# Linear attention and two MoE layers on one core: the top-2 gates computed once per 18 tiles instead of in groups of 6 and 3

## The chip, the cores and the metric

The kernel runs on one core of one Trainium2 chip. The metric is the device time of one execution in microseconds; the numbers shown are the median, lowest and highest of three runs, and one further execution was recorded by the profiler. Engines are named as in the profile: PE is TensorE, DVE is VectorE, ACT is ScalarE, POOL is GpSimd, SP is SyncE (it only issues DMAs here).

## What is computed

Linear attention for 8 batches of 8 heads, 576 positions and head size 64, then a top-2 mixture of 8 experts over the 4608 tokens, then a soft mixture. Cut to what matters here:

```python
x = softmax(q) @ (softmax_over_sequence(k).T @ v)        # per head; 4608 tokens x 512
logits = x @ w_gate                                       # 4608 x 8
noisy = logits + log1p(exp(x @ w_noise)) * noise
top2 = argpartition(-noisy, 2)[:, :2]; w = softmax(noisy[top2])
out[t] = sum over the two experts e of t: w * relu(x[t] @ w1[e]) @ w2[e]
# then moe2: soft slots over all tokens, 8 experts x 4 slots
```

The "gate" is the part from `noisy` to the sorted list of tokens for each expert: softplus, the two largest of eight, their weights, a running count for each expert, and a table that says which token stands at which place of which expert's list.

## The kernel before, in words

Tokens are handled in 36 tiles of 128, nine tiles for each of four pairs of batches (`TP` = 9). Tensors live in pools whose tiles have a fixed number of buffers; a second use of a one-buffer tile waits for the first use to end.

`attention` runs steps that two strings name. `FIRST` holds pairs 0, 1 and 2 and the kv product of pair 3; `MIX` holds the outputs of pair 3. `ou1.4` is the output of pair 1, tile 4 (matmuls into a `pv` tile in PSUM, line 308 or 312; evicted by DVE, lines 315 to 328, or with an `a` by ACT, line 324). `qt` transposes q, `kv` makes the kv product (lines 277 and 278), `qm` and `qs` are q's maximum and its subtraction (line 248 on DVE, line 255 mostly on POOL), `he1.2` adds the gate logits over heads for three tiles (line 336), `ga1.0` queues a gate, `pf` queues `plan_first`, `pl` queues `plan`, and each `bg` advances the queued work up to its next mark (a bare `yield`). The written order gives priorities; a planner of the compiler then fixes the order on each engine's queue, so that work may be issued well ahead of its place in the strings. Each engine then runs its queue strictly in that order.

A gate is a chain across four engines. Lines 350 to 370 make the noisy logits (DVE, ACT with exp and log, POOL). Lines 375 to 392 compare the eight values with each other, mask ties and count, so that the two largest get a 1 in `s16`. Lines 395 to 401 are matmuls that give each token its running number per expert, on top of the count `cnt` of all earlier groups. Lines 403 to 409 make the weights and store them to `xtab` in DRAM. Lines 412 to 428 turn numbers into a place (`af` column, `bf` row). Lines 436 to 455 build one-hot matrices of three tiles at a time (`ob` of 128 rows, with the token number multiplied in on line 437; `oa` of `8*T1` columns, line 445) and multiply them into the table; lines 460 to 465 add the result into `tab`. `T1` is the number of the last tile of the group, so `oa` is wider for later groups. Before the change each pair has a group of six tiles and one of three, and one PSUM bank (`pk`) serves the running numbers and the table of every group in turn.

`plan_first` (line 592) needs the whole table of pairs 0 and 1. It makes the index list for the first ten blocks of 256 rows (POOL, line 614) and the first two gathers (line 628). Then `experts` runs: in each block (lines 838 to 870) eight parts, each with one `split` of a weight into two halves (line 763, ACT then DVE), a `hidden` (line 796) or a `result` (line 826) on PE. `MIX` is stretched over the first 72 of the 80 parts of these ten blocks, and ends with `plan`, which needs the whole table and makes the index lists for all later blocks; blocks of 384 rows start after the tenth. The excerpt below is printed from the kernel.

```python
assert i < 2 or TP * (i - 2) + 6 in seen              # before pair i reuses lgr
bg.append(gate(i * TP + 6 * j, i * TP + 6 + 3 * j))   # ga i.j
while n_done < min(n_steps, n_steps * n_parts // SPREAD):   # MIX over the parts
```

## Time and profile before

| | |
|---|---|
| median of three runs | 1232.7 us (1230.85 to 1234.57) |
| the profiled execution's own time | 1234.64 us |
| its span, first to last instruction | 1232.9 us |
| busy: PE, DVE, ACT, POOL | 1148.2, 802.4, 580.7, 326.9 us |
| mean granted TensorE clock | 0.967 of full speed |

The span is what the trace covers; the rest of the profiled execution's time lies around it. Busy time is an average over stages that have different limits, so the stages are read one by one below.

### The profile page before, as it was taken

The numbers are of one execution on the slowest core, as the hardware profiler recorded it, in microseconds if no ns is written. First come the engines' busy times: TensorE is split into PE (matmuls) and PEld (weight loads), VectorE is DVE, ScalarE is ACT, GpSimd is POOL, SyncE is SP. The second block draws the span as 40 slices with busy tenths as digits, with TensorE's granted clock in tenths as the row PEclk, the third lists the DMA queues.
The fourth block names the chain that finished last, engine by engine and source line by source line (L and its number), as shares of the span: only waits on it lengthen the run. The fifth ranks groups of instructions, "written<-read, shape, count | busy, mean of one in ns | idle before, by whom it ended". The sixth has DMA issues, their size and how long they took to land. (4 is left out here: it accounts for less than half of the span.)

```text
span 1232.9 us, 21326 instructions
## 1 busy us (share of the span) xinstructions
PE 1148.2 (93%) x7808; PEld 997.7 (81%) x7808; DVE 802.4 (65%) x1493; ACT 580.7 (47%) x879; POOL 326.9 (27%) x376
## 2 busy tenths in 40 slices
PE   6776989999999999999999999999999999969994
PEld 5665878998888998889978998998998998956542
DVE  7889777678876665555556666666666666646653
ACT  3554666464444444434434454544444454424324
POOL 3353251343242322112222322322321321310000
PEclk9788899999999999999999999999999999988997
DMA  9847471796446475556668564563846353237797
GB/s 342 289 143 274 155 263 40 198 290 186 113 106 180 111 215 148 144 163 169 170 176 264 139 199 104 148 193 85 220 108 171 47 151 78 45 69 287 260 356 307
DMA packets 116107, 219.10 MB, mean 178 GB/s; under 512 B 13968, under 2 KB 54032, under 8 KB 111888
## 3 DMA queue, kind: packets, MB, share of 16 engines
q1 hardware_dynamic: 98944, 177.11, 41.8%
q0 software_dynamic: 17040, 40.44, 17.2%
q8 instruction: 67, 1.10, 0.4%
q14 instruction: 56, 0.46, 0.1%
HBM read 243.31 MB, written 49.70 MB: 238 GB/s over the span
## 5 line engine op out<-in xcount | busy, mean ns | idle before, releaser
L763 DVE TENSOR_TENSOR R1l<-ringS,R1h 128x1024 fp32r<-128x1024 f32 x96 | 117.8, 1227 | 102.7 <-ACT R1h L763 100.2
L763 DVE TENSOR_TENSOR R0l<-ringS,R0h 128x1024 fp32r<-128x1024 f32 x95 | 116.4, 1225 | 104.1 <-ACT R0h L763 103.5
L763 ACT ACTIVATE R1h<-ringS 128x1024 fp32r<-128x1024 f32 x96 | 101.7, 1060 | 141.0 <-PE py L826 85.0
L763 ACT ACTIVATE R0h<-ringS 128x1024 fp32r<-128x1024 f32 x95 | 100.8, 1061 | 138.4 <-PE py L826 75.3
L763 DVE TENSOR_TENSOR R2l<-ringS,R2h 128x1024 fp32r<-128x1024 f32 x91 | 111.4, 1225 | 81.2 <-ACT R2h L763 78.7
L763 ACT ACTIVATE R2h<-ringS 128x1024 fp32r<-128x1024 f32 x91 | 96.5, 1060 | 136.2 <-PE py L826 72.6
L796 PE MATMUL ph<-xh,R0h 128*128 128x256 f32 x400 | 113.3, 283 | 2.5 <-ACT R2h L763 2.4
L796 PE MATMUL ph<-xl,R0h 128*128 128x256 f32 x400 | 113.4, 283 | 0.0
L796 PE MATMUL ph<-xh,R0l 128*128 128x256 f32 x400 | 112.9, 282 | 0.0
L800 DVE SCALAR_TENSOR_TENSOR hl<-ph,hh 128x512 fp32r<-128x512 f32 x140 | 95.7, 684 | 24.0 <-ACT hh L799 24.0
L709 POOL DMA_INDIRECT xg<-xtab,pl_idx x40 | 49.2, 1229 | 216.7 <-DVE sc L786 198.1
L796 PE MATMUL ph<-xh,R2h 128*128 128x256 f32 x360 | 102.2, 284 | 1.9 <-DVE hl L800 1.9
L796 PE MATMUL ph<-xl,R2h 128*128 128x256 f32 x360 | 102.0, 283 | 0.5 <-DVE xl L783 0.5
L796 PE MATMUL ph<-xh,R2l 128*128 128x256 f32 x360 | 101.8, 283 | 0.0
L796 PE MATMUL ph<-xh,R1h 128*128 128x256 f32 x360 | 100.7, 280 | 0.2 <-DVE hl L800 0.2
L796 PE MATMUL ph<-xl,R1h 128*128 128x256 f32 x360 | 100.3, 279 | 0.0
L796 PE MATMUL ph<-xh,R1l 128*128 128x256 f32 x360 | 100.3, 279 | 0.0
L832 POOL DMA_INDIRECT x<-y,pl_idx x40 | 63.5, 1588 | 129.0 <-DVE y L831 118.9
L799 ACT ACTIVATE hh<-ph 128x512 fp32r<-128x512 f32 x140 | 81.6, 583 | 32.5 <-PE ph L796 32.5
L826 PE MATMUL py<-R1l,hh 128*128 128x512 f32 x200 | 79.7, 399 | 0.0
L796 PEld LDWEIGHTS ph<-xh,R0h 128*128 128x128 f32 x400 | 76.2, 191 | 3.8 <-ACT R2h L763 2.8
L826 PE MATMUL py<-R1h,hl 128*128 128x512 f32 x200 | 78.8, 395 | 0.0
(439 smaller groups left out, 3064.6 us busy)
## 6 DMA issues: line engine op xcount, KB each, us to landing
ringS<-in_moe_w_dram SPq DMA_DIRECT2D x292, 512.0 KB
ringA<-in_moe_w_dram SPq DMA_DIRECT2D x12, 1024.0 KB
ringA<-in_moe_w_dram SPq DMA_DIRECT2D x22, 512.0 KB
xtab<-xr SPq DMA_DIRECT2D x36, 256.0 KB
kt<-in_k_dram SPq DMA_DIRECT2D x8, 1024.0 KB
v<-in_v_dram SPq DMA_DIRECT2D x8, 1024.0 KB
x<-z SPq DMA_DIRECT2D x5, 1280.0 KB
ringS<-x SPq DMA_DIRECT2D x5, 1024.0 KB
```

The costliest lines, as they stand in the source:

```text
L709: k.nc.gpsimd.indirect_dma_start(out=x, out_offset=None, in_=k.xtab[:n], in_offset=bass.IndirectOffsetOnAxis(ap=idx, axis=0))
L763: turn[1:] = [nc.scalar.activation(r[0], f, AF.Copy), nc.vector.tensor_sub(r[1], f, r[0].bitcast(F32))]
L796: nc.tensor.matmul(ph[:, g, :], w[i][:, c, g * P:(g + 1) * P], x[:, c, :], start=n == 0, stop=n == 11)
L799: nc.scalar.activation(hh[:, fs, :], ph, AF.Relu)
L800: nc.vector.scalar_tensor_tensor(hl[:, fs, :], ph, 0.0, hh[:, fs, :].bitcast(F32), op0=ALU.max, op1=ALU.subtract)
L826: nc.tensor.matmul(py[s], a[h], w[i][:, f, :], start=u == 4 and f == n == 0, stop=u == 7 and f == 1 and n == 2)
L832: d = nc.gpsimd.indirect_dma_start(out=k.x2[:NTOK // 2] if b < NPA else k.x2, out_offset=bass.IndirectOffsetOnAxis(ap=at(b, s), axis=0), i ...
```

## The change

Both kernels do the same arithmetic on the same tokens. `gate(i)` now takes 18 tiles, two pairs, and is queued twice: `ga0` in `FIRST` after `he1.2`, `ga2` in `MIX` after `he3.2`. The 58 `bg` of `FIRST` become 31: none stands ahead of `ga0`, and behind it one follows nearly every step (`he1.2 ga0 bg qe2.2 bg kv2.0 bg km3.0 bg kv2.0 bg kt2.0 bg ...`), 26 of them ahead of `pf` and 5 behind it, the last after `ke3.1`. All other steps keep their order. `MIX` has 105 entries in place of 85, with the outputs of pair 3 in the first 25. `heads` writes its last sum into a new tile `ls` of 18 tiles. The comparison `ge` is made in fp16, and its mask is multiplied on DVE and no longer on POOL. The one-hot matrices are made three tiles at a time with two buffers, and the table is made in two halves of nine tiles; `oa` has 144 columns for all of the first gate and 288 for all of the second. Names such as `g0` let intermediate tiles share memory.

```diff
 NPA, NPB, NST, NTR = 10, 30, 14, 8
 TE = 36
 NSLOT = 32
-GT = 6
+
+GN, GT = 2 * TP, TP
...
 MIX = """
-ga2.0 ga2.1 qt3.0 bg bg bg bg bg ou3.0a qt3.1 bg bg bg qt3.2 bg ou3.1a bg qt3.3 ou3.2 bg qt3.4 bg he3.0 ou3.3 bg qt3.5 bg ou3.4 bg bg bg bg ze ze qt3.6 bg ze bg ou3.5a bg bg qt3.7 bg bg ze he3.1 ou3.6a bg ou3.7 qt3.8 ou3.8 bg bg bg bg bg bg bg he3.2 bg bg bg ga3.0 bg ga3.1 bg bg bg bg pl bg bg bg bg bg bg bg bg bg bg bg bg bg bg bg
+qt3.0 ou3.0a qt3.1 qt3.2 ou3.1a qt3.3 ou3.2 qt3.4 he3.0 ou3.3 qt3.5 ou3.4 ze ze qt3.6 ze ou3.5a qt3.7 ze he3.1 ou3.6a ou3.7 qt3.8 ou3.8 he3.2 ga2 bg bg bg bg bg bg bg bg bg bg bg bg bg bg bg bg bg bg bg bg bg bg bg bg bg bg bg bg bg bg bg bg bg bg bg bg bg bg bg bg bg bg bg bg bg bg bg bg bg bg bg bg bg bg bg bg bg bg bg bg bg bg bg bg bg bg bg bg bg bg pl bg bg bg bg bg bg bg bg
 """
...
-    k.tril = ap.tile([P, E, E], F32, name="tril")
-    nc.gpsimd.affine_select(out=k.tril, in_=k.ones[:, :64].rearrange("p (e f) -> p e f", e=E), pattern=[[1, E], [-1, E]], compare_op=ALU.is_gt, fill=0.0, base=0, channel_multiplier=0)
+    trf = ap.tile([P, E, E], F32, name="trf")
+    nc.gpsimd.affine_select(out=trf, in_=k.ones[:, :64].rearrange("p (e f) -> p e f", e=E), pattern=[[1, E], [-1, E]], compare_op=ALU.is_gt, fill=0.0, base=0, channel_multiplier=0)
+    k.tril = ap.tile([P, E, E], F16, name="tril")
+    nc.vector.tensor_copy(k.tril, trf)
...
         def heads(T0, T1, eng):
 
-            lr = lgrs[T0 // TP][:, T0 % TP:T0 % TP + T1 - T0]
-            for w in (4, 2, 1):
+            i, j = T0 // TP, T0 % TP
+            lr = lgrs[i][:, j:j + T1 - T0]
+            for w in (4, 2):
                 eng.tensor_add(lr[:, :, 0:w], lr[:, :, 0:w], lr[:, :, w:2 * w])
-
-        def gate(T0, T1):
-            n_t = T1 - T0
+            if i // 2 not in lss:
+                lss[i // 2] = sp.tile([P, GN, 2 * E], F32, name="ls")
+            j += i % 2 * TP
+            eng.tensor_add(lss[i // 2][:, j:j + T1 - T0], lr[:, :, 0], lr[:, :, 1])
+            seen.append(T0)
+
+        def gate(i):
+
+            T0, n_t = i * TP, GN
+            T1 = T0 + n_t
 
 
             n_c = E * T1
             cols = k.cols[:, :n_c]
             tabs = tab.rearrange("p (e c) -> p e c", e=E)[:, :, :T1]
-            full = lambda n, s=None, d=F32: sp.tile(s or [P, GT, E], d, name=n)[:, :n_t]
+            full = lambda n, s=None, d=F32: sp.tile(s or [P, GN, E], d, name=n)
             flat = lambda x: x.rearrange("p t e -> p (t e)")
-            lr = lgrs[T0 // TP][:, T0 % TP:T0 % TP + n_t]
-            z = lr[:, :, 0, E:]
-            na = full("na")
+            lr = lss[i // 2]
+            z = lr[:, :, E:]
+            na = full("g0")
             nc.vector.scalar_tensor_tensor(na, z, -1.0, z, op0=ALU.mult, op1=ALU.min)
-            u = full("u")
+            u = full("g1")
             nc.scalar.activation(u, na, AF.Exp)
...
-            n = sp.tile([P, GT, E], F32, name="n", bufs=2)[:, :n_t]
+            n = full("n")
             nc.gpsimd.tensor_mul(n, ln, noise[:, T0:T1, :])
-            nc.gpsimd.tensor_add(n, n, lr[:, :, 0, 0:E])
-            yield 1
-            seen.append(T0)
-
-            ge = full("ge", [P, GT, E, E])
+            nc.gpsimd.tensor_add(n, n, lr[:, :, 0:E])
+            yield
+
+            ge = full("ge", [P, GN, E, E], F16)
             nc.vector.tensor_tensor(ge, bcast(n, 2, E), bcast(n, 3, E), op=ALU.is_ge)
             yield 1
-            nc.gpsimd.tensor_tensor(ge, ge, bcast(k.tril, 1, n_t), op=ALU.mult)
-            m1 = full("m1", [P, GT])
+            nc.vector.tensor_tensor(ge, ge, bcast(k.tril, 1, n_t), op=ALU.mult)
+            m1 = full("m1", [P, GN])
             nc.vector.tensor_reduce(m1, n, axis=AX.X, op=ALU.max)
             nc.gpsimd.tensor_sub(n, n, bcast(m1, 2, E))
             nc.scalar.activation(n, n, AF.Exp)
             yield
...
-            pk = pr.tile([P, GT, E], F32, name="pk")[:, :n_t]
+            pk = pr.tile([P, GN, E], F32, name="pk")
...
-            ob = sp.tile([P, GT, P, 2], F16, name="ob")
-            parts = [slice(m, m + CW // 2) for m in range(0, n_t, CW // 2)]
             over = lambda x, ms, n: bcast(x[:, ms], 2, n)
-            for ms in parts:
-                n_p = ms.stop - ms.start
-                nc.vector.tensor_tensor(ob[:, ms], bcast(k.cols[:, :P], 1, n_p), over(bf, ms, P), op=ALU.is_equal)
-                nc.vector.tensor_tensor(ob[:, ms], ob[:, ms], over(k.tok1, ms, P), op=ALU.mult)
-                yield 1
-            yield
-            oas = []
-
-            def columns(ms):
-                n_p = ms.stop - ms.start
-                oas.append(sp.tile([P, CW // 2, E * TE, 2], F16, name="oa", bufs=2)[:, :n_p, :n_c])
-                nc.vector.tensor_tensor(oas[-1], bcast(cols, 1, n_p), over(af, ms, n_c), op=ALU.is_equal)
-
-            for ms in parts[:2]:
-                columns(ms)
-                yield 1
-            yield
-            pa = pr.tile([P, E, T1], F32, name="pk")
-            for ms in parts:
-                oa = oas.pop(0)
-                for m in range(2 * ms.start, 2 * ms.stop):
-                    nc.tensor.matmul(pa.rearrange("p e c -> p (e c)"), ob[:, m // 2, :, m % 2], oa[:, m // 2 - ms.start, :, m % 2], start=m == 0, stop=m == 2 * n_t - 1)
-                if len(oas) and ms.stop < n_t - CW // 2:
-                    columns(slice(ms.stop + CW // 2, ms.stop + CW))
+            for h in range(0, n_t, GT):
+                pa = pr.tile([P, E, T1], F32, name="pk")
+                for m0 in range(0, GT, CW // 2):
+                    ms, ml = slice(h + m0, h + m0 + CW // 2), slice(m0, m0 + CW // 2)
+                    ob = sp.tile([P, CW // 2, P, 2], F16, name="ob", bufs=2)
+                    nc.vector.tensor_tensor(ob, bcast(k.cols[:, :P], 1, CW // 2), over(bf, ms, P), op=ALU.is_equal)
+                    yield 1
+                    nc.vector.tensor_tensor(ob, ob, over(k.tok1, ml, P), op=ALU.mult)
+                    yield 1
+                    oa = sp.tile([P, CW // 2, E * TE, 2], F16, name="oa", bufs=2)[:, :, :n_c]
+                    nc.vector.tensor_tensor(oa, bcast(cols, 1, CW // 2), over(af, ms, n_c), op=ALU.is_equal)
+                    for m in range(CW):
+                        nc.tensor.matmul(pa.rearrange("p e c -> p (e c)"), ob[:, m // 2, :, m % 2], oa[:, m // 2, :, m % 2], start=m0 + m == 0, stop=m0 + CW // 2 == GT and m == CW - 1)
+                    yield
+                if T0 + h == 0:
+                    nc.vector.tensor_copy(tabs, pa)
+                else:
+                    tt = sp.tile([P, E * TE], F32, name="tt")[:, :n_c].rearrange("p (e c) -> p e c", e=E)
+                    nc.vector.tensor_scalar(tt, pa, 0.0, float((T0 + h) * P), op0=ALU.is_gt, op1=ALU.mult)
+                    nc.vector.tensor_add(tabs, tabs, pa)
+                    nc.vector.tensor_add(tabs, tabs, tt)
                 yield
-            if T0 == 0:
-                nc.vector.tensor_copy(tabs, pa)
-            else:
-                tt = sp.tile([P, E * TE], F32, name="tt")[:, :n_c].rearrange("p (e c) -> p e c", e=E)
-                nc.vector.tensor_scalar(tt, pa, 0.0, float(T0 * P), op0=ALU.is_gt, op1=ALU.mult)
-                nc.vector.tensor_add(tabs, tabs, pa)
-                nc.vector.tensor_add(tabs, tabs, tt)
...
-                bg.append(gate(i * TP + 6 * j, i * TP + 6 + 3 * j))
+                bg.append(gate(i))
```

## Rows read from the trace of the kernel before

**Rows 1.** Stretches: length, busy PE, PEld, DVE, ACT, POOL (instructions), PEclk, DMA, GB/s

```profile
106.00:131.00 25.00, 15.39 (x94) 12.77 (x93) 23.41 (x68) 12.31 (x29) 10.97 (x11) 0.66 0.69 249
131.00:143.00 12.00, 12.00 (x81) 10.06 (x82) 7.45 (x29) 4.76 (x7) 5.61 (x18) 1.00 0.65 231
143.00:169.00 26.00, 21.64 (x184) 19.49 (x185) 24.95 (x98) 20.60 (x58) 6.23 (x14) 1.00 0.34 123
169.00:182.00 13.00, 13.00 (x97) 11.06 (x96) 7.20 (x29) 7.25 (x17) 8.92 (x25) 1.00 0.93 310
182.00:194.00 12.00, 8.97 (x62) 8.00 (x62) 11.89 (x41) 6.82 (x12) 5.05 (x7) 0.86 0.47 150
194.00:250.00 56.00, 56.00 (x385) 51.59 (x384) 37.97 (x77) 28.86 (x50) 13.23 (x14) 1.00 0.45 124
...
300.00:345.00 45.00, 42.92 (x290) 38.71 (x289) 37.87 (x92) 22.86 (x29) 18.32 (x20) 1.00 0.46 113
...
445.00:625.00 180.00, 180.00 (x1185) 163.31 (x1185) 93.60 (x147) 74.03 (x116) 38.80 (x29) 1.00 0.58 159
```

**Rows 2.** Waits of PE, 60 to 131 us, by releaser: total us, times, longest

```profile
PE pv L312 <- DVE lgr L328: 4.3, 1, 4.3
PE pk L395 <- DVE tab L460: 3.4, 1, 3.4
PE pk L455 <- DVE ob L437: 2.2, 1, 2.2
PE pv L277 <- ACT xr L324: 2.0, 1, 2.0
```

**Rows 3.** Timeline of DVE: start, us, line; first and last gate instructions of four stretches

```profile
68.35 2.75 DVE L350 SCALAR_TENSOR_TENSOR na<-lgr 128x48 f32<-128x48 f32 x1 [0.38 <-POOL lgr L336]
...
130.15 0.44 DVE L362 RECIPROCAL rw<-w 128x48 f32<-128x48 f32 x1
...
168.62 0.29 DVE L465 TENSOR_TENSOR tab<-tab,tt 128x144 f32<-128x144 f32 x1
...
193.90 0.17 DVE L407 RECIPROCAL s<-s 128x3 f32<-128x3 f32 x1
...
337.06 0.45 DVE L465 TENSOR_TENSOR tab<-tab,tt 128x288 f32<-128x288 f32 x1
```

**Rows 4.** Timeline of POOL: a subtraction of q, gathers, the plan's last copy

```profile
68.27 2.76 POOL L255 TENSOR_TENSOR q<-q,qm 128x1536 f32<-128x1536 f32 x1
...
178.99 1.19 POOL L709 DMA_INDIRECT pl_x<-xtab,pl_ia  x1 [1.10 <-DMA ringS<-in_moe_w_dram]
...
355.15 0.18 POOL L688 COPY pl_id<-pl_idx 128x2 int32 x1 [0.27 <-POOL pl_idx L684]
...
420.57 1.02 POOL L709 DMA_INDIRECT xg<-xtab,pl_id  x1 [14.31 <-PE py L826]
```

**Rows 5.** Timeline of PE: outputs, the first gathered rows, the first expert matmul

```profile
95.52 1.27 PE L308 MATMUL pv<-KB,qT 128*128 128x162 f32 x8
...
118.05 2.53 PE L308 MATMUL pv<-KB,qT 128*128 128x162 f32 x8 [0.54 <-DVE lgr L328]
...
186.43 1.92 PE L781 MATMUL ph<-ident,pl_x 128*128 128x128 f32 x8
...
193.83 0.36 PE L796 MATMUL ph<-xh,R1h 128*128 128x256 f32 x1
```

**Rows 6.** Gate instructions of DVE by shape, to 445 us: busy us, mean ns

```profile
L437 DVE TENSOR_TENSOR ob<-ob,tok 128x768 f16<-128x768 f16 x12 | 6.7, 579 | 0.0
L387 DVE TENSOR_REDUCE r<-ge 128x48 f32<-128x384 f32 x4 | 3.4, 850 | 0.0
...
L387 DVE TENSOR_REDUCE r<-ge 128x24 f32<-128x192 f32 x4 | 2.0, 492 | 0.0
...
L445 DVE TENSOR_TENSOR oa<-cols,af 128x1728 f16<-128x1728 f16 x1 | 1.1, 1066 | 0.0
...
L445 DVE TENSOR_TENSOR oa<-cols,af 128x864 f16<-128x864 f16 x1 | 0.6, 594 | 0.0
```

More of the change, by code (lines that the diff above doesn't have):

```diff
@@ L146, in attention @@
         lgrs, rqas, seen = {}, {}, []
-        m8s = {}
+        m8s, lss = {}, {}
         tab = k.tab = ac.tile([P, E * TE], F32, name="tab")
@@ L344, in gate @@
             tabs = tab.rearrange("p (e c) -> p e c", e=E)[:, :, :T1]
-            full = lambda n, s=None, d=F32: sp.tile(s or [P, GT, E], d, name=n)[:, :n_t]
+            full = lambda n, s=None, d=F32: sp.tile(s or [P, GN, E], d, name=n)
             flat = lambda x: x.rearrange("p t e -> p (t e)")
-            lr = lgrs[T0 // TP][:, T0 % TP:T0 % TP + n_t]
-            z = lr[:, :, 0, E:]
-            na = full("na")
+            lr = lss[i // 2]
+            z = lr[:, :, E:]
+            na = full("g0")
             nc.vector.scalar_tensor_tensor(na, z, -1.0, z, op0=ALU.mult, op1=ALU.min)
-            u = full("u")
+            u = full("g1")
             nc.scalar.activation(u, na, AF.Exp)
-            w = full("w")
+            w = full("g2")
             nc.vector.tensor_scalar_add(w, u, 1.0)
@@ L357, in gate @@
             yield
-            dl = full("dl")
+            dl = full("g0")
             nc.vector.scalar_tensor_tensor(dl, w, -1.0, u, op0=ALU.add, op1=ALU.subtract)
-            rw = full("rw")
+            rw = full("g3")
             nc.vector.reciprocal(rw, w)
@@ L382, in gate @@
             yield
-            r1 = full("r1")
+            r1 = full("g1")
             nc.vector.tensor_reduce(r1, ge, axis=AX.X, op=ALU.add)
             yield
-            r2 = full("r2")
+            r2 = full("g2")
             nc.vector.tensor_reduce(r2, ge.rearrange("p t e f -> p t f e"), axis=AX.X, op=ALU.add)
-            yield 1
+            yield
             nc.vector.tensor_sub(r1, r1, r2)
@@ L403, in gate @@
             nc.gpsimd.tensor_mul(n, n, s16)
-            s = full("s", [P, GT])
+            s = full("s", [P, GN])
             nc.vector.tensor_reduce(s, n, axis=AX.X, op=ALU.add)
@@ L410, in gate @@
             yield
-            pos = full("pos")
+            pos = full("g0")
             nc.vector.scalar_tensor_tensor(pos, bcast(k.ef, 1, n_t), float(T1 * P), pk, op0=ALU.mult, op1=ALU.add)
             nc.vector.tensor_mul(pos, pos, s16)
-            pp = full("pp", [P, GT, 2])
+            pp = full("pp", [P, GN, 2])
             nc.vector.tensor_reduce(pp[:, :, 1], pos, axis=AX.X, op=ALU.max)
             yield 1
-            ps = full("ps", [P, GT])
+            ps = full("ps", [P, GN])
             nc.vector.tensor_reduce(ps, pos, axis=AX.X, op=ALU.add)
@@ L420, in gate @@
             yield
-            pi = full("pi", [P, GT, 2], I32)
+            pi = full("pi", [P, GN, 2], I32)
             nc.vector.tensor_copy(pi, pp)
-            ai = full("ai", [P, GT, 2], I32)
+            ai = full("ai", [P, GN, 2], I32)
             nc.vector.tensor_scalar(ai, pi, 7, None, op0=ALU.logical_shift_right)
-            af = full("af", [P, GT, 2], F16)
+            af = full("af", [P, GN, 2], F16)
             nc.vector.tensor_copy(af, ai)
-            bf = full("bf", [P, GT, 2], F16)
+            bf = full("bf", [P, GN, 2], F16)
```

4 lines of the change are left out of this document (2 added, 2 removed).

## The prediction

> **What bounds the kernel now.** I read the chain that ended last first. It can be followed back only to the start of the blocks of 256 rows behind 625 us, and there it is expert matmuls. The table of stretches fills in the rest: from 445 to 625 us PE is busy for all of its 180 us at full clock, and from 194 to 250 for all of 56 [rows 1]. So the end is set by when PE gets through the first ten blocks, and what happens after 445 us moves as a whole. Only idle PE, a slow PE clock or added PE work ahead of 445 us counts.
>
> Read in the same table, the attention stage is different. From 106 to 131 us PE is busy for 15.39 of 25 us, DVE for 23.41, and the granted clock is 0.66. Then PE is full in both kv products (131 to 143 and 169 to 182), where DVE has 7.45 of 12 and 7.20 of 13 us of work. Between them DVE is the full engine, with 24.95 of 26, and again from 182 to 194, with 11.89 of 12 [rows 1]. The stage is bound in turn by DVE, PE, DVE, PE, DVE.
>
> Next, the waits of PE show what the gate of pair 0 costs there. PE waits 2.2 us for a one-hot matrix and 3.4 us for the table before the PSUM bank is free, with outputs of pair 1 queued behind both. It waits 4.3 us for an eviction that stands in DVE's queue behind the first gate instruction, and 2.0 us for an ACT eviction whose factor stands behind another [rows 2]. That first gate instruction lasts 2.75 us for 48 elements [rows 3], as long as the POOL subtraction that started 0.08 us before it [rows 4]. The outputs that follow cost PE 2.53 us in place of 1.27 us [rows 5], at about half the clock: a granted 1.2 GHz where it was 2.4.
>
> **The change, part by part.** *DVE work.* Counting the gate's lines 350 to 465, DVE spends 27.6 us on 67 instructions up to the reciprocal at 130.15, 18.6 us on 64 from there to the table at 168.62, 14.1 us on 45 up to 193.90 and 26.6 us on 85 up to 337.06 [rows 3]. For a group of 18 tiles I take the slopes of the shapes. The second sum over `ge` grows by 0.358 us for three more tiles, so 0.850 + 4 x 0.358 = 2.28 us. A chunk of three tiles takes 0.58 + 0.58 + 0.594 = 1.75 us for `ob` twice and `oa` in the first gate, and 0.58 + 0.58 + 1.066 = 2.23 in the second [rows 6]; six chunks are 10.5 and 13.4 us. I put the other 25 small instructions at 10 us and the table at 1.1 and 2.7 us, an estimate on the same slopes. That makes about 24 us for the first gate and 28 us for the second. Ahead of the experts the gate's DVE work thus falls from 27.6 + 18.6 + 14.1 = 60.3 to about 24 us, since pair 2's gate is moved behind pair 3's outputs; behind their start it grows from 26.6 to about 28.
>
> *Up to the end of pair 1 (131 us).* All gate work leaves. The gate's share of the waits is 2.2 + 3.4 + 2.0, and of the 4.3 us the 2.7 that the blocked instruction took: 10.3 us. The slow clock added 1.26 us to each of three outputs; with half of that, 1.9, the stretch could shrink by 12. Other work is late next: from 106 to 131 DVE still has about 12 us (its 23.41 less some 11 that I count of the gate's 27.6), and the ACT evictions and POOL subtractions remain. I take -9 us. Bounds: -5, the waits for `ob` and half of the rest; -14, all of it and the whole clock loss.
>
> *From there to the experts.* The first gate's 24 us stands where 18.6 us of pair 1's stood: +5.4 us for DVE, plus waits of a chain that cannot overlap with another group of its own. The kv stretches can hide some: DVE idles 4.6 us in the first [rows 1]. I take +4 us, bounds 0 and +8. The first expert block hangs on the table: from it (168.62) to the gather 10.4 us, to the transposes of the gathered rows 17.8, to the first expert matmul 25.2 [rows 3 to 5]. In that last piece, 182 to 194, DVE is full, with pair 2's gate on it and PE idle for 3.0 us [rows 1]. Without that gate the splits come sooner: -2 us; bounds -5, and +3 if the longer chain has the table later than now and PE runs out of pair 3's outputs to fill with.
>
> *Behind the experts' start.* Six small groups of waits and table loads become one chain, but it can only use gaps of DVE, 18 of 56 us in the stretch from 194 [rows 1]. Pair 3's outputs move from some 50 parts to 17, because 25 of 105 entries come first; I put their nine evictions at 8 us of DVE, which those gaps hold. PE idles for 2.1 us in 300 to 345 where the small groups of the last gate and the plan run [rows 1]. Longer instructions (2.28 us against 0.85) stand between two splits, so I add 1.5 us; bounds -1 and +9. `plan` may end later: now its last copy is at 355.15 and the first gather that needs it at 420.57 [rows 4], so 65 us hide it. The written place of `pl`, entry 97 of 105, would be at part 67 of 80, near 395 us; even then the list would be 10 us ahead. If that cover went, each us late is a us of PE.
>
> *At nothing:* the matmuls of the gate. There are three fewer running-number matmuls a gate, and the table matmuls are as many but wider; PE has both hidden in a stage that DVE bounds, and behind the experts' start I put the difference of the two below 1 us. The extra cast of the mask is one DVE instruction near the start, where loads bound the stage. Stores to `xtab` fall from eight issues to two on SP, behind which weight loads queue; the fewer stand there the better, and I give that no gain.
>
> **A rule against the change.** POOL's mask is now a DVE multiply of two SBUF inputs, 1152 elements long. The Trainium skill, page "SBUF — State Buffer", section "Who interferes with whom", says that a VectorE instruction with two SBUF inputs and a GpSimd one that reads SBUF block each other for the whole instruction. The 2.75 us instruction, which reads two SBUF inputs, agrees with it [rows 3, 4]. By the rule the sum would be the first rival's, near +1.5 us; by the rows alone it is -5.5, since they don't show POOL at work where the new gate runs.
>
> **The sum.** -9 + 4 - 2 + 1.5 = -5.5 us. The profiled execution, 1234.64 us, would take 1229.1; it is 1.9 us above the median, so against that I forecast 1232.7 - 5.5 = 1227.2 us.
>
> **The rivals.** *Given back (same, 0.21).* What pair 1 gains goes into the longer chain: the table comes at 168 as now, for DVE work that was spread over 100 us is bunched, or the blocking moves along. Pair 3's three POOL subtractions, 2.76 us each in the row seen [rows 4], meet the new gate's front: 3 x 2.6 = 7.8 us on DVE. Then -9 + 4 - 2 + 1.5 + 7 = +1.5, about 1234. For it: the DVE is full between the kv products. Against: by then the subtractions are likely over. That the planner leaves the work where it was in time, so that the change does not do what it says, ends here too.
>
> *Slower through the expert blocks (0.14).* PE has two banks for `hidden`; an eviction late on DVE stops it. If the second gate's front and its six chunks, some twelve places, each leave PE idle for 0.9 us, the price is 11 us: -9 + 4 - 2 + 11 = +4, about 1237. It decides when PE idles over 7 us more behind the experts' start than its present few. For it: PE already idles there at 300 to 345. Against: none at all in 194 to 250 with DVE at 38 of 56 us.
>
> *Slower through a late table (0.07).* If the 18-tile chain has the table after 180 us, the experts start near 205 and the fill work of pair 3 cannot cover it: 1238.
>
> *More than forecast (0.12).* Both DVE-bound stretches shrink and nothing comes back: about -14, 1219.
>
> **Numbers.** The forecast has 0.46. A measurement of this kernel can tell about 0.3%, 3.7 us, from no change. Faster is 0.46 + 0.12 = 0.58, same 0.21, slower 0.21. The forecast's own range is 1222 to 1229. The range for 8 in 10 takes in the given-back case and the nearer slower ones and leaves out a late table and a gain above 14: 1219 to 1238.
>
> **What the changed profile would show.** Right: no gate instruction on DVE ahead of the last output of pair 1; that output some 9 us earlier; no waits of PE on `ob` or `tab` up to there and a clock above 0.66; the first expert matmul at 185 to 190; PE idle by no more than about 4 us from there to 445. Wrong: the table not before 168, or PE waiting for `hl` or `pv` evictions behind the experts' start. The prediction fails most easily if the planner puts the second half's outputs and gate in places that stop PE, since the row of before shows only short gate instructions there.

## The result and the profile after

The changed kernel is slower: 1249.78 us in the median of four runs (1248.01 to 1250.05), beside 1233.63 us for the kernel before on the same chip (1230.85 to 1236.63). The ratio is 1.0121, with a 95% interval of 1.0094 to 1.0147. Its profiled execution has a span of 1248.1 us (before 1232.9).

Both kernels end alike: from the first matmul of the blocks of 384 rows it is 783.4 us to the end before and 784.1 after. So the loss lies ahead of it, and the table of stretches is cut at the same events in both kernels: start and end of pair 2's kv product, start of pair 3's kv product, first expert matmul, first matmul of the blocks of 384 rows. Below they are called stretches A (from 60 us), kv, B, C and D. Before (a row: stretch, its length, busy us and instructions of each engine, granted clock, DMA):

```profile
core 0: us, PE busy (x) PEld busy (x) DVE busy (x) ACT busy (x) POOL busy (x), PEclk, DMA share, GB/s
60.00:130.86 70.86, 50.71 (x335) 43.49 (x333) 62.16 (x159) 38.96 (x85) 29.22 (x39) 0.81 0.59 207
130.86:142.50 11.64, 11.64 (x81) 9.82 (x79) 7.47 (x29) 4.76 (x7) 5.71 (x19) 1.00 0.66 239
142.50:168.74 26.24, 21.88 (x185) 19.61 (x184) 24.69 (x96) 20.35 (x57) 6.23 (x14) 1.00 0.34 119
168.74:193.80 25.06, 22.03 (x157) 19.11 (x155) 19.15 (x66) 14.32 (x30) 13.97 (x31) 0.93 0.72 237
193.80:449.50 255.70, 253.09 (x1684) 228.67 (x1683) 183.54 (x363) 131.91 (x193) 80.03 (x96) 1.00 0.57 160
```

After:

```profile
60.00:118.76 58.76, 42.64 (x282) 37.55 (x280) 40.73 (x89) 27.28 (x68) 21.30 (x21) 0.91 0.68 241
118.76:137.50 18.74, 18.74 (x107) 15.62 (x107) 5.33 (x13) 6.52 (x11) 2.56 (x8) 0.75 0.46 169
137.50:174.56 37.06, 25.71 (x199) 24.11 (x199) 33.03 (x97) 20.13 (x57) 11.50 (x17) 0.86 0.29 93
174.56:199.30 24.74, 21.67 (x131) 18.94 (x129) 10.32 (x28) 8.13 (x20) 7.53 (x16) 0.81 0.66 227
199.30:464.00 264.70, 258.42 (x1707) 232.42 (x1706) 185.96 (x322) 129.50 (x190) 80.19 (x86) 0.99 0.54 154
```

Stretch A became 12.1 us shorter, but kv, which now has output 1.8 in its middle, 7.1 us longer. B grew by 10.8, C fell by 0.3 and D grew by 9.0: together +14.5 us of the 15.2 by which the spans differ.

The same rows say what the time went to. Length less PE's busy time, summed, is 30.2 us of idle PE before and 36.8 after: +6.7. Busy time multiplied by what the clock lacks of 1 (50.71 x 0.19, 22.03 x 0.07; after it 42.64 x 0.09, 18.74 x 0.25, 25.71 x 0.14, 21.67 x 0.19, 258.42 x 0.01) is 11.2 us of slow clock before and 18.8 after: +7.6. This is rough, since the mean clock of a stretch counts its idle time too. The traces have the clock at 0.50 from 72.3 to 82.5, 113.2 to 130.3 and 184.9 to 188.3 us before, and from 73.6 to 77.0, 107.8 to 114.6, 118.0 to 128.2, 141.9 to 145.3, 152.1 to 159.0, 189.7 to 199.9 and 285.2 to 288.7 after. Half of PE's busy time in these is 10.1 us before and 18.9 after: +8.8. What remains, PE's work at full clock, then differs by 1 us. So idle PE and slow clock each make up about half of the loss.

**Stretch A.** The waits of PE from 60 to 140 us, as in [rows 2] (waiter, releaser, us in total, times, longest):

```profile
PE pv L280 <- issue: 4.5, 1, 4.5
PE pv L311 <- DVE lgr L331: 4.3, 2, 3.9
PE pv L280 <- ACT xr L327: 3.8, 1, 3.8
```

The waits for `ob` and for the table's bank are gone, but PE's idle time in A fell by only 4.0 us (20.15 to 16.12). The 3.8 us stand ahead of pair 1's kv product at 73 us, where the trace before has a wait of 2.0 [rows 2]. The other two, 3.9 and 4.5 us, stand just ahead of pair 2's. Timelines of DVE, POOL and PE there (start, duration):

```profile
106.45 1.75 DVE L251 TENSOR_REDUCE qm<-qt 128x24 f32<-128x1536 f32 x1 [0.73 <-DMA qt<-in_q_dram]
108.19 0.20 DVE L344 TENSOR_TENSOR ls<-lgr 128x48 f32<-128x48 f32 x1
109.20 0.28 DVE L331 TENSOR_TENSOR lgr<-pv,rqa 128x128 f32<-128x128 f32 x1
114.92 2.63 DVE L344 TENSOR_TENSOR ls<-lgr 128x48 f32<-128x48 f32 x1
117.77 0.69 DVE L330 TENSOR_TENSOR xr<-pv,rqa 128x512 f32<-128x512 f32 x1
114.73 2.76 POOL L258 TENSOR_TENSOR qt<-qt,qm 128x1536 f32<-128x1536 f32 x1
109.62 4.66 PE L311 MATMUL pv<-KB,qT 128*128 128x162 f32 x16 [3.93 <-DVE lgr L331]
118.76 2.06 PE L280 MATMUL pv<-v,kt 128*128 128x129 f32 x8 [4.48 <-issue]
```

The first wait is for an eviction that stands behind a maximum of q of 1.75 us, which itself had waited 0.73 us for its load. For the second the profile names no releaser; the eviction that starts at 117.77, and whose second instruction ends at 118.66, is the last thing ahead of it on DVE. It stands behind one row that is as odd as the 2.75 us row of [rows 3]: the same addition took 0.20 us at 108, started before POOL's subtraction, and 2.63 us at 115, started 0.19 us after one. The Trainium skill, page "SBUF — State Buffer", section "Who interferes with whom", says that a VectorE instruction with two SBUF inputs contends with a GpSimd one that reads SBUF, and this row agrees. In the trace before, three such subtractions in a row met an instruction of the gate instead (its eight executions have a median of 0.19 us):

```profile
121.63 1.92 DVE L413 TENSOR_TENSOR pos<-pos,s 128x24 f32<-128x24 f32 x1
115.16 8.34 POOL L255 TENSOR_TENSOR qt<-qt,qm 128x1536 f32<-128x1536 f32 x3 [7.31 <-DVE rqa L315]
```

So the blocking that the change took from the gate passed to the sum of the logits.

**Stretch kv.** TensorE's clock around its start:

```profile
114.00:118.00 4.00, 0.28 (x2) 0.00 (x0) 3.97 (x8) 0.56 (x3) 3.68 (x4) 0.93 0.60 222
118.00:122.00 4.00, 3.24 (x12) 2.82 (x13) 0.66 (x2) 4.00 (x10) 0.50 (x3) 0.50 0.73 269
122.00:126.00 4.00, 4.00 (x20) 3.25 (x20) 0.00 (x0) 0.20 (x1) 0.00 (x0) 0.50 0.64 237
126.00:130.00 4.00, 4.00 (x28) 3.15 (x24) 1.26 (x4) 0.00 (x0) 0.89 (x4) 0.72 0.04 16
130.00:134.00 4.00, 4.00 (x28) 3.29 (x27) 2.84 (x8) 1.70 (x3) 0.60 (x2) 1.00 0.83 311
```

PE idled for nearly all of 114 to 118 us, and then ran at the lower level, 0.50, for the first part of the kv product. Before, the kv product ran at 1.00 throughout [rows 1]: the lower level had come earlier, from 113.2 to 130.3 us, over the last outputs of pair 1. From 60 us to the end of this kv product the clock costs about the same in both, 8.4 and 8.8 us.

**Stretch B.** DVE's timeline through the new gate, from its first instruction to the table:

```profile
131.93 0.31 DVE L361 SCALAR_TENSOR_TENSOR g<-ls 128x144 f32<-128x144 f32 x1
...
143.25 0.75 DVE L387 TENSOR_TENSOR ge<-ge,tril 128x1152 f16<-128x1152 f16 x1
...
148.96 1.35 DVE L394 TENSOR_REDUCE g<-ge 128x144 f32<-128x1152 f16 x1
150.23 2.12 DVE L397 TENSOR_REDUCE g<-ge 128x144 f32<-128x1152 f16 x1
152.38 0.69 DVE L330 TENSOR_TENSOR xr<-pv,rqa 128x512 f32<-128x512 f32 x1
...
175.32 0.75 DVE L462 TENSOR_TENSOR tab<-tab,tt 128x144 f32<-128x144 f32 x1
```

The front starts 4.7 us later than that of pair 1's first group did (127.21 in the trace before), and the table ends at 176.1 us, in place of 168.9 [rows 3]. The longest wait of PE in this stretch, 6.0 us before it starts again at 153.4, is for a factor that DVE makes at 153.18; it stands behind the eviction at 152.38, and this behind the two sums. Of the 10.8 us by which B grew, 7.0 are idle PE (4.36 to 11.35) and 4.5 the clock, which was at full speed throughout before; PE's work is 0.6 less.

**Stretch D.** DVE's timeline, and PE's row that follows it:

```profile
280.24 1.34 DVE L394 TENSOR_REDUCE g<-ge 128x144 f32<-128x1152 f16 x1
281.51 2.16 DVE L397 TENSOR_REDUCE g<-ge 128x144 f32<-128x1152 f16 x1
283.58 1.21 DVE L761 TENSOR_TENSOR R2l<-ringS,R2h 128x1024 fp32r<-128x1024 f32 x1
284.72 0.68 DVE L781 TENSOR_TENSOR xl<-ph,xh 128x512 fp32r<-128x512 f32 x1
285.45 0.58 PE L794 MATMUL ph<-xl,R1h 128*128 128x256 f32 x1 [3.30 <-DVE xl L781]
```

The same two sums, now of the second gate, stand ahead of the `xl` that the next expert block needs, and PE waits 3.30 us for it. Its clock is 0.77 in the 6 us from 282.

### The profile page after: what moved, and what is told of

Same layout as the page of the kernel before. It is cut to its first block, busy times and chain, and to the rows that moved or that the text cites. A ratio compares the mean times of both kernels' runs of the same rounds, so it can differ in the third digit from the quotient of the medians.

```text
span 1248.1 us, 21055 instructions
## 1 busy us (share of the span) xinstructions
PE 1157.3 (93%) x7802; PEld 1006.8 (81%) x7802; DVE 782.4 (63%) x1334; ACT 561.9 (45%) x849; POOL 314.9 (25%) x326
## 5 line engine op out<-in xcount | busy, mean ns | idle before, releaser
L797 ACT ACTIVATE hh<-ph 128x512 fp32r<-128x512 f32 x140 | 81.7, 584 | 32.5 <-PE ph L794 32.5
```

The lines of the kernel that those rows point to most:

```text
L797: nc.scalar.activation(hh[:, fs, :], ph, AF.Relu)
```

## The experiments

All medians are beside runs of the kernel before on the same chip (1233.6 to 1236.0 us), to which the ratios refer. Runs on different chips are compared by their ratios. In the edits `gb i.j` is a gate of six or three tiles, `gc i` one of nine tiles, `ga i` one of 18, all made by the new code; the edits are shortened. The times of first18, mix18, nine, mix9end, late9 and late9h lie outside the ranges of either of their theories, so what they tell rests on the stretches.

**1 to 4. Which half: old groups in one half, or in both.**

```diff
first18: FIRST as changed          MIX as before, with gb2.0 gb2.1 ... gb3.0 ... gb3.1
mix18:   FIRST as before, with gb  MIX as changed
ctl63:   both as before, with gb
ctl63n:  ctl63, each intermediate tile with a buffer of its own
```

> Only the first half is changed: one 18-tile gate after the last output of pair 1, old strings and groups of six and three for pairs 2 and 3. Theory one, two separate losses: the trace has +5.5 us at the first expert matmul and +9 us behind it, so this alone is at 1237 to 1241 us, with the long stretch between the two kv products (36 us against 25) seen again. Rival, all of the loss follows from the first half (a late start that drags the fill work behind it): 1246 or more. Second rival, all of it sits in the second half: 1230 to 1235.

> Only the second half is changed: old strings and groups up to the experts, then pair 3's outputs first and one 18-tile gate behind them. Theory one: the +9 us behind the first expert matmul appear here, 1240 to 1244 us, with PE idle by 5 to 7 us between the first expert matmul and the tenth block's end in place of 2.6. Rival, the loss belongs to the first half: 1230 to 1236.

> The new gate code (logits summed into one tile, fp16 comparison, mask on DVE, one-hot matrices three tiles at a time) with the old groups of six and three and the old strings. If the loss comes from grouping and placement, as the two traces suggest, this stands within 0.4% of before, 1229 to 1238 us. Rival: the new instruction forms themselves cost time (mask on DVE, three-tile chunks in a new order); then this is at 1240 or more.

> The control of groups of six and three again, now with a buffer of its own for each intermediate tile and two for n, as the kernel before has. If the control's 1255 us came from the second group of a pair waiting for the first group's shared tiles, this falls to 1230 to 1240 us. Rival, the new instruction forms (three-tile chunks, mask on DVE) lose time in small groups: it stays above 1248.

| | median us | ratio (95%) | first expert matmul | D |
|---|---|---|---|---|
| first18 | 1243.05 | 1.0073 (1.0038 to 1.0108) | 200.9 | 257.3 |
| mix18 | 1259.18 | 1.0192 (1.0145 to 1.0239) | 219.0 | 257.9 |
| ctl63 | 1254.88 | 1.0151 (1.0102 to 1.0200) | 220.5 | 251.2 |
| ctl63n | 1250.91 | 1.0112 (1.0085 to 1.0139) | 214.5 | 251.9 |

first18 puts about half of the loss, or a little more, into the first half: its ratio is 1.0073 with late experts, the changed kernel's 1.0121, and its D is 7.4 us shorter than the changed kernel's. The control missed: old groups at the old places, in the new code, lost as much as the change or more, ahead of the experts. So mix18 and ctl63 tell only the difference in D, +6.7 us for 18 tiles in the second half. Separate buffers, a cause that I tried, are no clear gain: the ratio fell from 1.0151 to 1.0112, with intervals that overlap.

**5. The control with its marks counted.** The new code has one mark more in a group, so that the same number of `bg` gets less far.

```diff
             nc.gpsimd.tensor_add(n, n, lr[:, :, 0:E])
-            yield
+            yield 1
```

> The control with the new gate code in groups of six and three at the old places, with one mark of the gate's code less, so that a group has 9 or 8 marks to be stepped over as in the kernel before, and not 10 or 9. If the control lost its 15 to 19 us because the written steps no longer got through the groups and the first plan before the experts, the first expert matmul comes at 192 to 197 (the control: 220.5) and the time is 1234 to 1240. Rival, the rewritten instructions themselves (the mask on DVE, the 18-tile sums of logits, the shared buffers) cost it: 1249 to 1255, first expert matmul behind 210.

1245.29 us, ratio 1.0072 (1.0047 to 1.0096), first expert matmul at 205.8. Neither theory: the mark explains some 10 us of the control's loss, and about as many remain (pair 2's kv product starts at 140.4, with a wait of PE of 11.0 us for an eviction ahead of it). The control is not a clean one and is used for nothing else.

**6 to 8. Nine tiles.**

```diff
nine:       gc0 ... gc1 in FIRST, gc2 ... gc3 in MIX, each where its pair's group of six was queued
nine_late2: nine, with gc2 behind he3.0
mix9end:    FIRST as changed;  MIX: -ga2  +gc2 gc3
```

> One gate of nine tiles for each pair, in the old places of the groups of six and three, so larger groups without waiting for a second pair. If the waiting for the second pair (bunching) is what costs, and not the size, this is 1225 to 1234 us. Rival, longer instructions cost by themselves: 1238 or more.

> Nine tiles a gate, and pair 2's gate moved from the head of the second string to behind he3.0, so out of the last kv product's stretch, where in the run of nine the comparison and sums of pair 2 stand ahead of the last KB copies and the first weight splits. If that is what holds the experts there (193.3 us, 15 us behind the kv product), they start at 186 to 189 us and the total is 1228 to 1233, below before. Rival, the work only moves behind the first expert matmul, where PE has no gap either: 1235 to 1238.

> The changed kernel, but with two gates of nine tiles behind pair 3's outputs in place of one of 18. If the second half loses by the length of the instructions (the two sums of 1.3 and 2.2 us ahead of an eviction), the 3.3 us wait of PE shrinks and this is 3 to 5 us faster than the changed kernel, 1245 to 1247. Rival, it loses because all gate work of two pairs and pair 3's outputs come behind the first expert matmul: 1248 to 1252, no gain.

nine takes 1236.17 us (ratio 1.0011, 0.9991 to 1.0032) and nine_late2 1236.56 (1.0007, 0.9990 to 1.0024): the new code with one gate for each pair is as fast as before, so the rewritten instructions alone need not lose anything. mix9end takes 1244.17 (1.0064, 1.0043 to 1.0086), with D at 257.9: nine tiles in the second half give back 6.8 us there. But pair 2's gate moved with it: its first instruction ran at 174.5 us, ahead of the experts.

**9. The wide instructions of the first gate behind the evictions.** hold18 wrote the `bg` of these steps behind output 2.0; held wrote them behind output 2.1 and put ordering edges on DVE.

```diff
+            with tc.issue_after(ev[2, 1].ins):     # DVE's last eviction of output 2.1
                 nc.vector.tensor_tensor(ge, ...); ... mask, r1 and r2 alike
```

> The changed kernel with the comparison, the two sums and all that follows written behind ou2.0, two steps between attention steps, so that they stand behind the evictions of pair 2's first outputs. If these wide gate instructions ahead of the evictions cost the stretch between the kv products its 11 us, PE's 6 us wait is gone and the second kv product starts by 168 to 171 us in place of 174.6. Theory one then expects the table later and the first expert matmul no earlier than 197, so the total is within 4 us of the changed kernel, 1246 to 1253. Rival, only the order mattered and nothing else hangs on the table: 1240 to 1244.

> The changed kernel, with the comparison, its mask and the two sums of the first gate (5.6 us of DVE) put by an ordering edge behind DVE's last eviction instruction of output 2.1, so that they can no longer stand ahead of the evictions of outputs 2.0 and 2.1. If these four instructions cost the 6 us wait of PE behind pair 2's kv product and the wait is the loss, the stretch between the two kv products falls from 37.1 to 31 to 33 us, the first expert matmul comes at 194 to 196 and the time is 1243 to 1246. Rival, the chain of the gate is what counts and the wait only shows where it is paid: the stretch falls as much, but the table comes later than 176 and the first expert matmul stays at 198 to 201, time 1247 to 1251.

In hold18 (1248.08, ratio 1.0105, 1.0081 to 1.0129) the order on DVE stayed that of the changed kernel, since the planner places work by what it needs and not by where it is written; it tells nothing. In held (1251.22, 1.0128, 1.0089 to 1.0168) the edges hold. PE's waits between its two kv products, 135.7 to 175.8 us:

```profile
PE pk L411 <- DVE s L408: 5.5, 1, 5.5
PE pk L460 <- DVE ob L455: 2.5, 2, 2.0
PE pv L311 <- DVE lgr L331: 1.1, 1, 1.1
```

All but 1.1 us of the wait for the eviction is gone, and one of 5.5 us for `s16` has taken its place: the running-number matmuls stand in PE's queue ahead of the next outputs. B is 40.1 us long, which neither theory had, but the first expert matmul, 199.7, is in the rival's range and the time 0.2 us above it: the wait only showed where the chain is paid.

**10. Nine tiles at the changed places.**

```diff
-ga0      (behind he1.2)          -ga2      (behind he3.2)
+gc0 gc1                          +gc2 gc3
```

> The changed kernel, with two gates of nine tiles each queued where the changed kernel queues one of 18: the first two behind the last output of pair 1, the other two behind the last of pair 3. If the size of a group is the cost in the first half as it was in the second (there nine tiles gave back 5.6 us), the stretch between the kv products falls from 37.1 to 30 to 33 us and the time is 1237 to 1241. Rival, the waiting for the second pair is the cost, whatever the size, since all gate work of two pairs then falls between the two kv products: that stretch stays at 35 to 38 us, the first expert matmul at 197 to 200, and the time is 1243 to 1246, that of the kernel with nine tiles in the second half alone.

1235.88 us, ratio 1.0001 (0.9983 to 1.0020): all of the loss is gone. But DVE's timeline shows where pair 0's gate ran, and pair 1's to the table:

```profile
77.49 0.23 DVE L361 SCALAR_TENSOR_TENSOR g<-ls 128x72 f32<-128x72 f32 x1 [4.97 <-POOL ls L344]
...
132.67 0.23 DVE L361 SCALAR_TENSOR_TENSOR g<-ls 128x72 f32<-128x72 f32 x1 [1.53 <-POOL ls L344]
...
163.83 0.31 DVE L463 TENSOR_TENSOR tab<-tab,tt 128x144 f32<-128x144 f32 x1
```

Written behind pair 1's last output, pair 0's gate started at 77 us, as soon as its logits were there. So this run changed two things, the size and the waiting for the second pair. Its rows for kv and B:

```profile
129.70:142.70 13.00, 13.00 (x93) 11.19 (x91) 8.01 (x19) 4.52 (x7) 3.21 (x10) 1.00 0.64 237
142.70:167.90 25.20, 20.70 (x172) 18.43 (x172) 22.24 (x84) 18.37 (x54) 8.76 (x18) 1.00 0.43 144
```

**11 and 12. The two things apart.**

```diff
late9h:   late9, the first instruction of gc0 behind DVE's eviction of output 1.8
late9h2:  late9, the first instruction of gc2 behind DVE's eviction of output 3.8
+            with tc.issue_after(ev[1, 8].ins):
                 nc.vector.scalar_tensor_tensor(na, z, -1.0, z, op0=ALU.mult, op1=ALU.min)
```

> The kernel with two gates of nine tiles behind each second pair, in which the trace showed pair 0's gate on DVE at 77 to 120 us although it is written behind pair 1's last output: here its first instruction has an ordering edge behind DVE's eviction of output 1.8, so that both gates of the first half must run behind it, still nine tiles each. If waiting for the second pair is the cost (11 us of DVE work more in the one stretch where DVE is full), the stretch between the kv products is 35 to 38 us long (25.2 without the edge), the kv product of pair 2 starts at 116 to 120, and the time is 1241 to 1246. If the size of the group is the cost (one chain of 18 that cannot overlap with another), two chains of nine give most of it back: that stretch 28 to 33 us, the time 1235 to 1240.

> The same two gates of nine tiles, with pair 2's gate held behind DVE's eviction of output 3.8 instead (its first half is that of the kernel without edges). In that one DVE had 16.7 us of work between the start of pair 3's kv product and the first expert matmul, in the changed kernel 10.3. If waiting for the second pair is the cost, the stretch from the first expert matmul to the blocks of 384 rows grows from 258.3 to 262 to 266 us and the time to 1240 to 1244. If the size is, it stays at 257 to 260 and the time at 1234 to 1238.

late9h takes 1247.41 us, ratio 1.0102 (1.0052 to 1.0151). Its rows for kv and B, and the start and the end of its two gates:

```profile
119.14:136.50 17.36, 17.36 (x96) 14.36 (x97) 5.83 (x18) 6.79 (x11) 3.31 (x11) 0.73 0.49 183
136.50:176.47 39.97, 27.68 (x213) 24.87 (x210) 34.91 (x120) 22.69 (x60) 9.71 (x21) 0.79 0.29 93
```

```profile
129.49 0.22 DVE L362 SCALAR_TENSOR_TENSOR g<-ls 128x72 f32<-128x72 f32 x1
...
175.81 0.30 DVE L464 TENSOR_TENSOR tab<-tab,tt 128x144 f32<-128x144 f32 x1
```

With groups of nine, but none before pair 1's end, the first half looks as with 18: the kv product starts at 119 and runs at a clock of 0.73, B is 40 us long, and the table ends at 176.1, as in the changed kernel. The first expert matmul comes at 204.2 (late9: 193.3). So in the first half it is the waiting for the second pair that costs, not the size. What it costs is mostly clock. From 60 us to the first expert matmul, in late9 and in late9h:

```profile
60.00:193.34 133.34, 103.77 (x739) 90.45 (x738) 100.70 (x277) 67.93 (x161) 45.78 (x76) 0.90 0.58 198
60.00:204.23 144.23, 111.75 (x739) 97.91 (x738) 100.25 (x283) 69.12 (x166) 44.92 (x77) 0.83 0.53 183
```

PE idles for 29.6 and 32.5 us, only 2.9 more, but the same 739 matmuls keep it busy for 103.8 and 111.8 us, 8.0 more. In late9 most of the idle time lies ahead of pair 2's kv product (22.3 us of it), and the kv product and B run at full clock; in late9h 12.3 us of it lie in B, and both run slow: the clock is at 0.50 for 48 us of these 144, in late9 for 28 of 133.

late9h2 takes 1235.30 us (1.0005, 0.9980 to 1.0029) with D at 258.1, though its second half too has both gates behind the experts' start (from 258 us). In the second half it is the size.

**13. The two sums in halves.** Each sum as two instructions of nine tiles, in both gates of the changed kernel.

```diff
-            nc.vector.tensor_reduce(r1, ge, axis=AX.X, op=ALU.add)
+            hs = (slice(0, TP), slice(TP, GN))
+            for x in hs:
+                nc.vector.tensor_reduce(r1[:, x], ge[:, x], axis=AX.X, op=ALU.add)      # r2 alike
```

> The changed kernel with each of the two sums over the comparison, in both gates, made in two instructions of nine tiles in place of one of 18 (0.7 and 1.1 us in place of 1.35 and 2.15), everything else as it is. If single long instructions ahead of what PE waits for are the cost, the stretch from the first expert matmul to the first matmul of blocks of 384 rows falls from 264.7 to 260 to 262 us, and the time to 1243 to 1247. Rival, the chain and its bunched total count, not the length of one instruction: that stretch stays at 263.5 to 266 and the time at 1248 to 1251.

1249.72 us (1.0115, 1.0081 to 1.0149), D 264.3: nothing. The four halves stood back to back on DVE, still ahead of `xl`, and PE waited 3.4 us. Not the length of one instruction, but that of the block.

**14. The two sums of the second gate behind `xl`.**

```diff
+            with tc.issue_after(k.xl.ins):         # the xl that PE waited 3.3 us for
                 nc.vector.tensor_reduce(r1, ...); nc.vector.tensor_reduce(r2, ...)
```

> The changed kernel with the two sums over the second gate's comparison (1.34 and 2.16 us) moved by an ordering edge on DVE from ahead of a weight split and the subtraction xl that PE waited 3.3 us for to just behind that xl. Nothing else is moved. Theory: in the second half the cost of 18 tiles is that these two sums stand as one block of 3.5 us ahead of what PE needs, and the lower clock that follows PE's wait: the stretch from the first expert matmul to the blocks of 384 rows falls from 264.7 to 259 to 262 us, the time to 1244 to 1248. Rival: the block costs as much wherever it stands, since PE then waits for the results' eviction or the hidden rows behind it: the stretch stays at 263.5 to 266, the time at 1248 to 1251.

1244.30 us, ratio 1.0062 (1.0040 to 1.0084). D's row and DVE's timeline:

```profile
197.80:457.20 259.40, 256.44 (x1706) 230.02 (x1705) 185.86 (x322) 129.44 (x189) 85.61 (x86) 1.00 0.56 157
```

```profile
279.78 0.68 DVE L787 TENSOR_TENSOR xl<-ph,xh 128x512 fp32r<-128x512 f32 x1
...
280.47 1.35 DVE L399 TENSOR_REDUCE g<-ge 128x144 f32<-128x1152 f16 x1
281.73 2.19 DVE L403 TENSOR_REDUCE g<-ge 128x144 f32<-128x1152 f16 x1
```

Two instructions of 3.5 us, moved from ahead of a split of 1.2 us and an `xl` of 0.7 us to behind them, give back 5.3 us of D: 3.3 of idle PE, the rest nearly all the clock, which is 1.00 again. That is most of what nine tiles gave back (6.6 to 6.8).

**15 to 17. What DVE work costs.** Four sums of 1.33 us that nothing reads, added to the changed kernel.

```diff
more_early: written behind outputs 1.0 to 1.3      more_late: between the kv products, behind outputs of pair 2
more_late2: with ordering edges behind DVE's evictions of outputs 2.0, 2.1 and twice 2.3
+                nc.vector.tensor_reduce(jo, ji, axis=AX.X, op=ALU.add)
```

> The changed kernel with four idle sums over a constant (1152 elements in, 144 out, 1.35 us each as the gate's first sum; nothing reads them) written behind outputs 1.0, 1.1, 1.2 and 1.3: 5.4 us of DVE work in the stretch that the change emptied. Theory, that stretch has room on DVE and gate work there cost little: time 0 to 2 us above the changed kernel, 1248 to 1252. Rival, a us of DVE work costs the same on either side of pair 2's kv product: 4 to 6 us above, 1253 to 1257.

> The same four idle sums written between the two kv products instead, behind the transposes of q of output 2.2 and behind outputs 2.0, 2.1 and 2.2. Theory, this stretch is bound by DVE (33.0 of its 37.1 us busy), and each us of work costs a us: 3.5 to 6 us above the changed kernel, 1253 to 1257. Rival, it is bound by the gate's chain and its waits, and what is beside the chain is hidden in the 4 us that DVE idles: 0 to 2 us above, 1248 to 1252.

> The changed kernel with four idle sums on DVE (1152 elements in, 144 out, about 1.33 us each; nothing reads them), each with an ordering edge that keeps it behind DVE's evictions of outputs 2.0, 2.1 and 2.3 (two behind the last), so that they fall between the two kv products. Theory, that stretch is bound by DVE: the 5.3 us lengthen it from 37.1 to 41 to 43 us, time 1253 to 1257. Rival, it is bound by the chain of the gate and by PE's waits, and DVE's 4 idle us take most of the added work: 37 to 39 us, time 1249 to 1252.

The first two took 1255.19 (1.0173, 1.0124 to 1.0222) and 1254.95 us (1.0170, 1.0121 to 1.0219), and tell nothing of the question: without an input to wait for, the sums ran at 7 to 15 us in both. With edges (and a constant of the kernel as input) they ran at 149 to 160 us:

```profile
135.20:171.65 36.45, 25.20 (x187) 23.16 (x186) 35.54 (x96) 19.76 (x56) 10.98 (x17) 0.86 0.29 91
```

B did not grow, nor did C (24.8 us), and the time is 1250.76 us (1.0127, 1.0088 to 1.0165). That interval is too wide to tell by itself, as it holds most of my theory's range; the stretch tells. My theory fell: B isn't bound by the amount of DVE's work, though DVE is busy for 35.5 of its 36.5 us. 5.4 us beside the gate's chain are hidden, some of them because other work of DVE moved behind B (it is busy for only 2.5 us more); what isn't hidden is what PE waits for.

No version beat the kernel before; late9h2, nine, nine_late2 and late9 equal it.

## Why the prediction was wrong

**What it had right.** The end is set by PE ahead of the blocks of 384 rows. The gate's DVE work is 24.5 us in 48 instructions for the first gate (estimated 24) and 27.9 in 50 for the second (28); the longest sum takes 2.12 to 2.16 us (2.28). No gate work runs ahead of pair 1's end. `plan` stays covered: its last copy is at 357.5 us, and PE waits for nothing of it up to 464.

**Where the sum went wrong.** Forecast -5.5, in the stretches +14.5, so 20 us off: 4.0 up to the end of pair 2's kv product, 6.8 from there to pair 3's, 1.7 in the piece to the first expert matmul, and 7.5 behind it.

**Up to the end of pair 1, -9.** Stretch A lost 12.1 us, but output 1.8 and a kv product at 0.75 of the clock give 7.1 of it back: -5.0 at the kv product's end, the near bound. (As described, the waits for `ob` and half of the rest, this bound comes to 6.3 and not 5.) I took the 10.3 us of the gate's waits as gone, but PE's idle time fell by 4.0: PE then waited for evictions behind a maximum of q and behind the blocked addition. I had named ACT evictions and POOL subtractions as next; the subtractions did come, by way of DVE. The slow clock, which I had counted only as something to gain, moved from the outputs into the kv product (8.4 us up to its end before, 8.8 after).

**From there to the experts, +4: the step that failed.** It measured +10.8, beyond its bound of +8. I added DVE work (+5.4) and took off DVE's idle time, as if the stretch were a sum. The work was sized right, and more_late2 shows that the sum isn't what counts. What counts is that the whole of the chain now starts behind pair 1's last logits: late9 and late9h differ only in whether pair 0's gate may start at 77 us, and B in 25.2 against 40.0 us. Gate work done early was not free: in late9 pair 2's kv product starts at 129.7, in late9h at 119.1. But the first expert matmul comes at 193.3 against 204.2, and of these 10.9 us 2.9 are idle PE and 8.0 are the same matmuls at a lower clock (0.83 against 0.90). I gave this stretch no term for the clock at all. Which of PE's waits shows the chain depends on the order (an eviction in the changed kernel, `s16` in held, a one-hot matrix for 4.6 us in late9h). I had put the gate's matmuls at nothing because PE had time for them; they are short, but in held PE stood at them for 5.5 us, with transposes and outputs behind them in its queue. Which wait each fall of the clock belongs to wasn't separated by a run.

**The last piece, -2.** It measured -0.3. DVE is empty there as forecast (10.3 us of work against 19.2), but PE's idle time is the same 3.1 us, so pair 2's gate was not what kept PE idle there. PE has 26 matmuls fewer, and a clock of 0.81 against 0.93 takes back most of what they gave.

**Behind the experts' start, +1.5: the term that was mis-sized.** It measured +9.0, its upper bound. The mechanism was named (longer instructions between two splits), its size was not: one block of 3.5 us, one wait of 3.3, the clock after it (held2), and some 3 us of PE's work that ran ahead of the experts before, pair 2's gate among it (in held2, at full clock, PE is busy for 256.4 us of D, before for 253.1). I had priced it by the idle PE of [rows 1], where the same sums are short. With nine tiles, or with the two sums out of the way, 2 to 4 us of it are left (D from 257.9 to 259.4 against 255.7).

**Other readings of the prediction.** Its counts of DVE's work for pair 2's gate and the last one (14.1 us on 45, 26.6 on 85) are too high by one and two instructions; the trace has 14.0 on 44 and 26.1 on 83, which moves no term. The first gather that uses the list of `plan` is not the one at 420.57 but one at 356.13, right behind the list. Part 67 of 80 lies near 405 us and not 395, by the 255.7 us of the 80 parts. Where the prediction has loads bound the stage near the start, more_early says otherwise: there 5.3 us of DVE work put pair 0's kv product 5.4 us later.

**The rivals.** The stage of the slower one was right; not twelve places but one did it, and splitr shows that it is the block. Its own sign, over 7 us more of idle PE behind the experts' start, did not come: it is 3.7 us more, and the rest is clock and moved work. The table came late, 7 us later than before, but at 176 us, short of the 180 that I had set. I gave the two rivals 0.14 and 0.07 as if one excluded the other. They sit in different stages and add up, so their sum, beyond 1238, had no place in the range. In the first rival, three subtractions were to meet the gate's front; the front ran in 0.31 us instructions at 132 us, and the blocking hit the logits' sum at 115. The mask's multiplication, 0.75 us, met none, so what was weighed there against the change did not decide.

## What to carry to other kernels

Before a chain's early half is moved to its late half, ask what the early half covered: work that seems to cost waits where it stands can still be cheaper there than behind the last input. Price a longer instruction by what stands behind it in its engine's queue, and by the TensorE clock after the wait, not by its share of busy time. Rivals in different stages are added, not chosen from. And look in the trace whether an experiment moved what it meant to move: here hold18, late9 and the first two idle-sum runs did not, and an ordering edge did.

## What was not expected of the hardware

An addition of 48 elements took 0.20 us or 2.63 us by whether a POOL subtraction was running when it started. The clock's share of the loss, 8.8 us, is larger than the idle time's, 6.7 us; in late9h the same matmuls take 8.0 us longer than in late9, beside 2.9 us more of idle time. Taking away a wait of 3.3 us gave back 5.3. Four idle sums at 7 to 15 us, where DVE is busy for 16.0 of the first 20 us in the changed kernel, put pair 0's kv product at 20.45 us in place of 15.03; the two medians with them are some 5 us above the changed kernel's, though their intervals overlap its. At 149 to 160 us, in a stretch where DVE is nearly always busy, the same sums left the stretch as long as it was.
